# Re-measured durations, overlaps and delays in a kernel's list schedule, with exponentials and sines planned in pieces

## The chip, the cores and the metric

The kernel runs on one core of a Trainium2 chip. Its engines are TensorE (PE in the profile, with PEld for its weight loads), VectorE (DVE), ScalarE (ACT), GpSimd (POOL, which here only issues transfers) and SyncE (SP, which issues the other transfers); 16 DMA engines move the data. The metric is the device time in microseconds (us), as the median of several runs.

## The reference

Two branches over the same 2048 tokens of 512 channels are mixed by a gate for each token.

```python
g = sigmoid((x * gate_w).sum(-1, keepdims=True))
return g * a + (1 - g) * b

# a: a diagonal state-space layer (S4D) as a long convolution, 128 states a channel
dt = exp(log_dt)
A = -exp(log_A_real) + 1j * A_imag
C = (C_real + 1j * C_imag) * dt[:, None]
P = exp((A * dt[:, None])[:, :, None] * arange(2048))
K = 2.0 * einsum("dn,dnl->dl", C, P).real
a = irfft(rfft(u_t, 4096) * rfft(K, 4096))[:, :, :2048] + u * D_skip   # transposed

# b: a bilinear feed-forward layer of 1792 hidden channels
b = ((x @ w_gate) * (x @ w_up)) @ w_down
```

Everything is float32. B_x is not used: both branches take A_u.

## The kernel before, in words

**The feed-forward branch (GLU).** Each float32 factor is split into a rounded high part and a rest (xhi and xlo, whi and wlo, hh and hl, dhi and dlo), and a product is three matmuls, a *triple*, of 128x128 by 128x512 (`product` and `down`). The hidden channels are 14 tiles of 128, in five groups; the tokens are four chunks of 512. For each group and chunk, `hidden` makes a tile: eight triples into the accumulators pg and pu, a copy of pg to h on ACT, h = pu * h on DVE, hh = rounded h on ACT, hl = h - hh on DVE. `down` multiplies hh and hl by the down weights into y, and `evacuate` scales y on ACT into acc, which is added to the output by a transfer that POOL issues. There are 56 hidden steps and 672 triples.

**The state-space branch.** Channels go in 16 blocks of 32. For a block, `amplitudes` makes 21 real exponentials (one ACT operation for each of 21 powers, for two blocks at a time, into the tile e) and `phases` makes sines and cosines: on DVE the phase t, on ACT its rounding rt, on DVE the rest, and on ACT an absolute value and two sines. Their products on DVE (`direct_powers`, `leads`, `x_table`, `v_table`) are tables of powers x and v, whose matmuls on PE (`k_block`, its task `kgen`) give 2048 values of the convolution's kernel for each channel. Both it and the input go through a Fourier transform of two steps made of small matmuls (`u_part`, `k_first`, `m_second`), are multiplied on DVE (`m_product`), and come back in two steps (`m_inverse`, `m_last`), with transfers to memory and back between the steps. Four blocks make a quarter of the channels, after which `transforms` runs for this quarter.

**The order of the work.** Nothing is issued as it is written. Every function adds *tasks* to a list: the engine, a planned duration in us, the instructions, the tiles read and written, a rank (lower goes first), perhaps an earliest time `after`, and for a transfer its size. `Work.run` (lines 216 to 265) is a list scheduler: again and again it takes the task that can start earliest, at equal starts the one of lower rank, then of lower number, and moves the engine's planned time on by the duration. A task can start when its inputs have ended, plus a delay (`inputs`, lines 187 to 195), and when the buffers that it needs have been left by their users, plus the same delay (`slots`). The delay is 0.7 us for a task of PE and 0.15 us for the others, and nothing between two tasks of one engine:

```python
LAG = {"pe": 0.7}
lag = self.LAG.get(task.engine, 0.15)
at = max(at, d.end + (lag if d.engine != task.engine else 0.0))
```

At the end the tasks are issued in that order, and each engine then runs its own in order, whatever the real times are. Planned durations thus decide the order alone. Hidden steps are released one every `T_STEP` = 10.3 us of planned time and have rank 2 on PE; copies and products between them on ACT and DVE have rank 0; the state-space tasks have rank 1, some 0 or -1.

The 21 exponentials are one task of `1.3 + 21 * (0.13 + 0.0021 * 32 * blocks)` us (line 754), and the absolute value and the two sines are one task of 3.6 or 2.3 us (line 776). Exponentials and sines need different tables in ACT, which an ACT_TABLE_LOAD exchanges.

The operations go through one recorder, so that the profile has line 98 for all of them; they are told apart by their tiles (out<-in).

Of the kernel before, what the change touches and what calls it, by code (L numbers as in the profile page):

```python
# [13 lines left out]
AF = mybir.ActivationFunctionType  # L14
# [6 lines left out]
KT = D // P  # L21
# [6 lines left out]
TWO_PI = 2.0 * math.pi  # L28
# [4 lines left out]
NP = len(POWERS)  # L33

TURNS = [-l for l in POWERS[:11]] + POWERS[11:]
TB = 32
# [106 lines left out]
class Work:  # L143
# [7 lines left out]

    LAG = {"pe": 0.7}
    DMA_RATE = 0.3
# [10 lines left out]
    def add(self, engine, us, fn, r=(), w=(), rank=1, after=0.0, dma=0, hold=(), rows=()):  # L164
# [20 lines left out]
        return task  # L185

    def inputs(self, task):

        lag = self.LAG.get(task.engine, 0.15)
        at = task.after  # L190
        for d in task.deps:
            if d.end is None:
                return None
            at = max(at, d.end + (lag if d.engine != task.engine else 0.0))
        return at

    def slots(self, task, at):

        lag = self.LAG.get(task.engine, 0.15)
        taken = {}  # L200
        for tile in task.tiles:
            if tile.made is not None:
                continue
            n = taken.get(tile.key, 0)
            taken[tile.key] = n + 1
            place = len(tile.had) + n
            if not tile.loose and tile.turn != place:
                return None
            if place >= tile.bufs:
                for d in tile.had[place - tile.bufs].users:  # L210
                    if d.end is None:
                        return None
                    at = max(at, d.end + (lag if d.engine != task.engine else 0.0))
        return at

    def run(self):
# [5 lines left out]
        while any(left.values()):  # L222
# [29 lines left out]
            t.start, t.end = start, start + t.us  # L252
            free[t.engine] = t.end
            if t.dma:
# [14 lines left out]
def gated_mix_kernel(  # L269
# [20 lines left out]
    add = work.add  # L290
# [292 lines left out]
    def u_part(c):  # L583
# [159 lines left out]
    def amplitudes(bs):  # L743

        if bs[0]:
            pars.update(parameters(bs))
        par, rates = pars[bs[0]][2]
        e = new("tab", "e", [P, 2 * TB, NP])

        def exps():  # L750
            for k, l in enumerate(POWERS):
                act.activation(e.t[:, : TB * len(bs), k].rearrange("p (n d) -> p n d", d=TB), rates(), AF.Exp, scale=float(l))

        add("act", 1.3 + NP * (0.13 + 0.0021 * TB * len(bs)), exps, r=[par], w=[e])
        for n, b in enumerate(bs):
            amps[b] = e, lambda n=n: e.t[:, TB * n : TB * (n + 1)]

    def phases(b):
# [11 lines left out]

        def sines():
            act.activation(rt.t, t.t, AF.Abs)
            act.activation(t.t, t.t, AF.Sin, scale=-TWO_PI)
            act.activation(rt.t, rt.t, AF.Sin, scale=-TWO_PI, bias=half_pi[:, 0:1])

        add("act", 3.6 if b % 2 or not b else 2.3, sines, r=[m_const], w=[t, rt])
        polar[b] = t, rt
# [19 lines left out]
    def leads(b):  # L797
# [3 lines left out]
        par, C = pars[b][1]  # L801
        add("act", 0.42, lambda: act.copy(x.t[:, :, :, 0], C()), r=[par], w=[(x, ("l", 2))])
        q = new("tab", "sq", [P, 2, 2, TB, 3])
# [57 lines left out]
    def v_table(b):  # L861
# [7 lines left out]

        add("act", 1.3, copies, r=[ri], w=[(v, 2)])  # L870
        outer(
# [4 lines left out]
        for to, of, n in ((32, 0, 16), (56, 32, 8)):  # L876
# [11 lines left out]
            us = 0.04 * n + 0.08  # L888
            add("act", 2 * us - 0.2, sq_act, r=src_parts, w=[(v, ("r", k)), sq])
            add(  # L890
# [11 lines left out]
    def k_block(b, x, v):  # L902
# [26 lines left out]
    def k_first(q, kt):  # L929

        tt(0.19, lambda: kt.t[:, 48, :], lambda: kt.t[:, 48, :], lambda: skip[:, q], ALU.add, [m_skip], [kt])
        for h in range(2):
# [16 lines left out]

            add("pe", 2.1, fn, r=[kt, m_w1k], w=banks, rank=-1, hold=sts)  # L950
            for half in range(2):
# [58 lines left out]
    def m_second(q, ins, w):  # L1010
# [17 lines left out]

        add("pe", 2.1, fn, r=[*ins, w], w=banks[0] + banks[1], rank=1, hold=tos)
        for which in range(2):  # L1030
# [39 lines left out]
    def m_inverse(q, T, y, w):  # L1070
# [13 lines left out]

        add("pe", 1.15, fn, r=[y, w], w=banks, rank=1, hold=[ts])
        for j in range(4):
# [14 lines left out]
    def m_last(q, half):  # L1101
# [30 lines left out]

        add("pe", 1.9, fn, r=src, w=banks, rank=1, hold=fins)
        for i, f in enumerate(banks):
# [14 lines left out]

            args = ("dve", 0.69, mix_dve) if q == KT - 1 else ("act", 1.2, mix_act)  # L1150
            add(*args, r=[f, (m_gate, r // 4)], w=[(fin, i)])
# [119 lines left out]
```

## Time and profile before

| | |
|---|---|
| runs before, median | 632.51 us (631.53 to 634.56, three runs) |
| profiled execution, its own time | 633.44 us |
| its span, first to last instruction | 631.7 us |
| PE busy | 612.6 us, 97% |
| DVE busy | 495.4 us, 78% |
| ACT busy | 399.6 us, 63% |
| mean granted TensorE clock | 0.997 |

The profile is of one execution. Busy time of PE counts from the first to the modelled end of each matmul, and matmuls overlap, so that gaps of up to 0.16 us between matmuls don't show as idle. In the rows, "y<-dhi,hl" is an operation that writes y and reads dhi and hl; "k" is any accumulator of the state-space branch; the number after x is how many instructions a row holds; brackets at the end of a row give the idle time of the engine before it and what ended it, where "issue" means nothing that the profile shows.

### The profile page before, as it was taken

The page shows a single profiled execution, that of the slowest core. Times are in us where ns is not written, and L with a number is a line of the kernel's source. Part 1 is how long each engine was busy: PE and PEld are TensorE (multiplying, and loading weights), DVE is VectorE, ACT ScalarE, POOL GpSimd, SP SyncE. Part 2 cuts the span into 40 slices and gives each one's busy share as a digit, 9 for nine tenths or more (in the row PEclk, how much of TensorE's full clock was granted, in tenths as well). Part 3 has the DMA queues.
Part 4 walks back from the last instruction along what each step waited for, and adds up shares of the span by engine and source line. Part 5 has one row for each costly group of instructions (what it writes and reads, how often), then busy time and mean ns, then how long its engine had stood idle before and what let it go on. Part 6 is the DMA issues. An engine that isn't in the chain of part 4 may idle for free.

```text
span 631.7 us, 18000 instructions
## 1 busy us (share of the span) xinstructions
PE 612.6 (97%) x7526; PEld 468.8 (74%) x7526; DVE 495.4 (78%) x764; ACT 399.6 (63%) x931; POOL 106.1 (17%) x157
## 2 busy tenths in 40 slices
PE   8989999999999999999999999999999999998996
PEld 5667677678688887787778778768887887776783
DVE  6958999989969899799778898977998872146524
ACT  4477877885876795668687765785786543333320
POOL 3231523111021021002110202030101011130101
PEclk9999999999999999999999999999999999999998
DMA  8896949559779599578988959597979699897956
GB/s 309 295 335 248 328 136 369 178 159 287 190 183 300 148 242 274 136 217 190 260 196 199 292 159 247 156 190 190 276 165 265 184 255 252 285 248 206 239 129 116
DMA packets 111893, 142.64 MB, mean 226 GB/s; under 512 B 7876, under 2 KB 66756, under 8 KB 111556
## 3 DMA queue, kind: packets, MB, share of 16 engines
q1 hardware_dynamic: 90100, 105.05, 52.7%
q0 software_dynamic: 21568, 36.45, 28.0%
q8 instruction: 59, 0.97, 0.6%
q14 instruction: 22, 0.18, 0.1%
q10 hardware_dynamic: 144, 0.00, 0.0%
HBM read 81.96 MB, written 59.51 MB: 224 GB/s over the span
## 4 chain that ended last, share of the span: by engine, by line
PE 81%; issue 7%; DVE 5%; DMA 4%; POOL 1%; ACT 1%; POOLq 0%
PE y L98 22%; PE pg L98 20%; PE pu L98 20%; PE k L98 19%; DMA x_d<-xhi 2%; DVE x L98 2%; DMA su_d<-ts 1%; DVE v L98 1%; POOL x_d L98 1%; DMA y<-in_xT 1%; DVE m L98 1%; POOL su_d L98 0%; DVE hl L98 0%; DVE wlo L98 0%; DVE ri L98 0%
## 5 line engine op out<-in xcount | busy, mean ns | idle before, releaser
L98 POOL DMA_DIRECT2D out<-acc x60 | 51.5, 916 | 372.2 <-ACT acc L98 341.7
L98 PE MATMUL y<-dhi,hl 128*128 128x512 f32 x224 | 91.4, 408 | 3.8 <-DVE hl L98 3.5
L98 PE MATMUL pg<-xhi,wlo 128*128 128x512 f32 x224 | 90.3, 403 | 3.6 <-ACT h L98 1.5
L98 PE MATMUL pu<-xhi,wlo 128*128 128x512 f32 x224 | 89.7, 400 | 0.6 <-DVE h L98 0.6
L98 PE MATMUL pg<-xlo,whi 128*128 128x512 f32 x224 | 87.6, 391 | 0.1
L98 PE MATMUL y<-dlo,hh 128*128 128x512 f32 x224 | 87.5, 391 | 0.0
L98 PE MATMUL pg<-xhi,whi 128*128 128x512 f32 x224 | 87.5, 390 | 0.0
L98 PE MATMUL y<-dhi,hh 128*128 128x512 f32 x224 | 87.4, 390 | 0.0
L98 PE MATMUL pu<-xlo,whi 128*128 128x512 f32 x224 | 87.4, 390 | 0.0
L98 PE MATMUL pu<-xhi,whi 128*128 128x512 f32 x224 | 87.3, 390 | 0.0
L98 DVE TENSOR_TENSOR h<-pu,h 128x512 f32<-128x512 f32 x56 | 38.6, 689 | 55.9 <-PE pu L98 36.1
L98 ACT ACTIVATE acc<-y,ngate 128x512 f32<-128x512 f32 x76 | 51.5, 686 | 36.5 <-PE y L98 28.9
L98 ACT CAST hh<-h 128x512 fp32r<-128x512 f32 x56 | 34.7, 621 | 57.5 <-DVE h L98 57.5
L98 ACT COPY ts<-k 128x256 f32<-128x256 f32 (+1 forms) x144 | 51.2, 435 | 21.3 <-PE k L98 21.3
L98 PEld LDWEIGHTS y<-dhi,hl 128*128 128x128 f32 x224 | 42.0, 187 | 24.5 <-issue 7.9
L98 PEld LDWEIGHTS pg<-xhi,wlo 128*128 128x128 f32 x224 | 42.0, 187 | 21.0 <-issue 5.0
L98 ACT COPY h<-pg 128x512 f32<-128x512 f32 x56 | 32.9, 588 | 37.7 <-PE pg L98 25.3
L98 PEld LDWEIGHTS pu<-xhi,wlo 128*128 128x128 f32 x224 | 42.0, 188 | 14.8 <-issue 4.7
L98 PEld LDWEIGHTS y<-dhi,hh 128*128 128x128 f32 x224 | 42.1, 188 | 9.3
L98 PEld LDWEIGHTS pg<-xhi,whi 128*128 128x128 f32 x224 | 42.0, 188 | 9.1
L98 PEld LDWEIGHTS pu<-xhi,whi 128*128 128x128 f32 x224 | 42.1, 188 | 9.1
L98 PEld LDWEIGHTS pg<-xlo,whi 128*128 128x128 f32 x224 | 42.1, 188 | 8.6 <-DVE xlo L98 0.5
(105 smaller groups left out, 1128.6 us busy)
## 6 DMA issues: line engine op xcount, KB each, us to landing
out<-acc POOLq DMA_DIRECT2D x60, 256.0 KB, 6.3
xhi<-x_d SPq DMA_DIRECT2D x48, 256.0 KB, 5.1
xlo<-x_d SPq DMA_DIRECT2D x48, 256.0 KB, 5.2
raw<-in_wts SPq DMA_DIRECT2D x36, 256.0 KB, 4.6
su_d<-ts POOLq DMA_DIRECT2D x32, 256.0 KB, 6.2
sk_d<-ts SPq DMA_DIRECT2D x16, 512.0 KB, 5.7
y_d<-ts SPq DMA_DIRECT2D x16, 512.0 KB, 5.0
in<-sk_d SPq DMA_DIRECT2D x12, 512.0 KB, 7.4
```

What stands on the lines that cost most here:

```text
L98: got = getattr(self.engine, name)(*args, **kw)
```

## The change

No instruction is added, removed or altered; only the planner's numbers and the size of some tasks change, and with them the order. A dependence now costs nothing between two tasks of PE; otherwise 0.06 us for a task of PE, 0.3 for one of SP or POOL and 0.03 for ACT and DVE (now also behind a task of the same engine), and 0.17 more behind a task of PE. ACT and DVE are taken to be free 0.09 and 0.08 us before a task's end. The durations of PE's tasks and of some of ACT's are new. The 21 exponentials become three tasks of seven, and the absolute value and the two sines three tasks.

```diff
-    LAG = {"pe": 0.7}
+    LAG = {"pe": 0.06, "sp": 0.3, "pool": 0.3}
+    PE_LAG = 0.17
+    OVERLAP = {"act": 0.09, "dve": 0.08}
...
+    def ready(self, task, d):
+        if d.engine == task.engine == "pe":
+            return d.end
+        return d.end + self.LAG.get(task.engine, 0.03) + (self.PE_LAG if d.engine == "pe" else 0.0)
...
-            at = max(at, d.end + (lag if d.engine != task.engine else 0.0))
+            at = max(at, self.ready(task, d))
...
-            free[t.engine] = t.end
+            free[t.engine] = t.end - self.OVERLAP.get(t.engine, 0.0)
...
-        add("pe", 0.69, fn, r=[(w[0], which), (w[1], which), x[0], x[1]], w=[pg], rank=2, after=after)
+        add("pe", 0.681, fn, r=[(w[0], which), (w[1], which), x[0], x[1]], w=[pg], rank=2, after=after)
...
-        add("pe", 0.69, fn, r=[*h, *w], w=[y], rank=2)
+        add("pe", 0.681, fn, r=[*h, *w], w=[y], rank=2)
...
-        add("pe", 2.0, fn, r=[ut, m_w1], w=banks[0] + banks[1], rank=1, hold=sts)
+        add("pe", 2.08, fn, r=[ut, m_w1], w=banks[0] + banks[1], rank=1, hold=sts)
...
-        def exps():
-            for k, l in enumerate(POWERS):
-                act.activation(e.t[:, : TB * len(bs), k].rearrange("p (n d) -> p n d", d=TB), rates(), AF.Exp, scale=float(l))
-        add("act", 1.3 + NP * (0.13 + 0.0021 * TB * len(bs)), exps, r=[par], w=[e])
+        def exps(ks):
+            for k in ks:
+                act.activation(
+                    e.t[:, : TB * len(bs), k].rearrange("p (n d) -> p n d", d=TB), rates(), AF.Exp, scale=float(POWERS[k])
+                )
+        for n in range(3):
+            ks = range(7 * n, 7 * n + 7)
+            add("act", 0.17 + 1.29 * (n == 0) + 7 * (0.09 + 0.0009 * TB * len(bs)), lambda ks=ks: exps(ks), r=[par], w=[(e, n)])
...
-        add("act", 3.6 if b % 2 or not b else 2.3, sines, r=[m_const], w=[t, rt])
+        add("act", 0.77, lambda: act.activation(rt.t, t.t, AF.Abs), r=[t], w=[rt])
+        add(
+            "act", 2.13 if b % 2 or not b else 0.83, lambda: act.activation(t.t, t.t, AF.Sin, scale=-TWO_PI), w=[t],
+        )
+        add(
+            "act", 0.83, lambda: act.activation(rt.t, rt.t, AF.Sin, scale=-TWO_PI, bias=half_pi[:, 0:1]), r=[m_const],
+            w=[rt],
+        )
...
-        add("pe", 2.07, kgen, r=[x, v], w=[pk], rank=0, hold=[kt])
+        add("pe", 2.15, kgen, r=[x, v], w=[pk], rank=0, hold=[kt])
```

The other tasks of PE go from 2.1 to 2.08 (`k_first`), from 2.1 to 2.13 (`m_second`), from 1.15 to 1.27 (`m_inverse`) and from 1.9 to 2.0 (`m_last`); three more of ACT's fall by 0.02 to 0.11 us, and the two pairs of squares go from 1.24 and 0.6 to 1.15 and 0.73.

More of the change, by code (lines that the diff above doesn't have):

```diff
@@ L212, in slots @@
                         return None
-                    at = max(at, d.end + (lag if d.engine != task.engine else 0.0))
+                    at = max(at, self.ready(task, d))
         return at
@@ L801, in leads @@
         par, C = pars[b][1]
-        add("act", 0.42, lambda: act.copy(x.t[:, :, :, 0], C()), r=[par], w=[(x, ("l", 2))])
+        add("act", 0.31, lambda: act.copy(x.t[:, :, :, 0], C()), r=[par], w=[(x, ("l", 2))])
         q = new("tab", "sq", [P, 2, 2, TB, 3])
@@ L868, in copies @@
                 act.copy(v.t[:, c, :, 49:56], ri.t[:, c, :, W_A])
-        add("act", 1.3, copies, r=[ri], w=[(v, 2)])
+        add("act", 1.28, copies, r=[ri], w=[(v, 2)])
         outer(
@@ L888, in v_table @@
             us = 0.04 * n + 0.08
-            add("act", 2 * us - 0.2, sq_act, r=src_parts, w=[(v, ("r", k)), sq])
+            add("act", 1.15 if n == 16 else 0.73, sq_act, r=src_parts, w=[(v, ("r", k)), sq])
             add(
@@ L948, in fn @@
                     to += n
-            add("pe", 2.1, fn, r=[kt, m_w1k], w=banks, rank=-1, hold=sts)
+            add("pe", 2.08, fn, r=[kt, m_w1k], w=banks, rank=-1, hold=sts)
             for half in range(2):
@@ L1027, in fn @@
                                 )
-        add("pe", 2.1, fn, r=[*ins, w], w=banks[0] + banks[1], rank=1, hold=tos)
+        add("pe", 2.13, fn, r=[*ins, w], w=banks[0] + banks[1], rank=1, hold=tos)
         for which in range(2):
@@ L1083, in fn @@
                             )
-        add("pe", 1.15, fn, r=[y, w], w=banks, rank=1, hold=[ts])
+        add("pe", 1.27, fn, r=[y, w], w=banks, rank=1, hold=[ts])
         for j in range(4):
@@ L1131, in fn @@
                     )
-        add("pe", 1.9, fn, r=src, w=banks, rank=1, hold=fins)
+        add("pe", 2.0, fn, r=src, w=banks, rank=1, hold=fins)
         for i, f in enumerate(banks):
```

8 lines of the change are left out of this document (1 added, 7 removed).

## The prediction

> **What bounds the kernel now.** I read the page first, for the engines' shares and the chain.
>
> ```profile
> span 631.7 us, 18000 instructions
> ...
> PE 612.6 (97%) x7526; PEld 468.8 (74%) x7526; DVE 495.4 (78%) x764; ACT 399.6 (63%) x931; POOL 106.1 (17%) x157
> ...
> PE 81%; issue 7%; DVE 5%; DMA 4%; POOL 1%; ACT 1%; POOLq 0%
> ```
>
> TensorE (PE) is busy 97% of the span and holds 81% of the chain, so time can only come from gaps on PE. The second view, busy time by stretches, says where they are.
>
> ```profile
> 50.00:100.00 50.00, 48.18 (x324) 35.38 (x323) 46.62 (x79) 39.84 (x87) 15.49 (x24) 1.00 0.67 239
> 100.00:150.00 50.00, 48.73 (x446) 36.21 (x445) 46.19 (x75) 39.77 (x89) 10.05 (x14) 1.00 0.70 229
> 250.00:300.00 50.00, 50.00 (x676) 38.67 (x668) 44.49 (x60) 35.96 (x89) 5.83 (x6) 1.00 0.71 183
> 500.00:550.00 50.00, 50.00 (x538) 38.30 (x528) 23.12 (x35) 20.51 (x47) 4.12 (x5) 1.00 0.90 260
> ```
>
> The columns are PE, weight load, DVE (VectorE), ACT (ScalarE) and POOL. Early, PE lacks 1 to 2 us in 50, while DVE is at 92%; later PE is full, and the granted clock is 1.00 throughout. The chain and the timeline then give the exact size of a gap. In a full stretch twelve matmuls take 2.72 us, 0.227 us from start to start, although each is recorded 0.39 long; so a gap is the distance of two starts less 0.227, and is 0.16 us more than the idle time printed.
>
> ```profile
> 608.30 2.72 PE pg L98 x12
> ...
> 620.72 5.00 PE y L98 x21
> ```
>
> I went through the starts of all matmuls. After the first 20 us the gaps over 0.4 us are of two kinds. Seven, all before 170 us, end with a result of DVE or ACT. Five, later, end with nothing that the profile names; they lie inside or beside blocks of very many small matmuls, such as these:
>
> ```profile
> 376.64 0.43 PE L98 MATMUL k<-v,x 128*32 128x64 f32 x10 [0.56 <-issue]
> ...
> 584.76 0.69 PE L98 MATMUL k<-y,w3s 32*64 32x128 f32 x29 [1.46 <-issue]
> ...
> q8 instruction: 59, 0.97, 0.6%
> ```
>
> PE has 2 x 7526 instructions and queue q8 carried 59 blocks of them, one per some 255; a block of 128 small matmuls with 128 weight loads uses one up in 2 us. That the five gaps (0.84, 1.19, 0.76, 1.41, 1.71 us; 5.9 in all) are late instruction blocks is a reading, not shown. No planned duration changes how many instructions PE runs, so I leave them as they are.
>
> **The change part by part.** The program adds no arithmetic and takes none away; the same instructions are issued in another order. So every part is worth what it does to the seven gaps, and to gaps that are not there yet.
>
> First the exponentials in pieces. The largest gap:
>
> ```profile
> 108.48 0.69 DVE L98 TENSOR_TENSOR h<-pu,h 128x512 f32<-128x512 f32 x1 [0.56 <-PE pu L98]
> ...
> 109.68 1.28 ACT L98 ACT_TABLE_LOAD   x1
> 110.97 3.27 ACT L98 ACTIVATE e<-pb 128x64 f32<-128x64 f32 x21
> 114.07 0.61 ACT L98 CAST hh<-h 128x512 fp32r<-128x512 f32 x1
> ...
> 113.74 1.09 DVE L98 TENSOR_TENSOR x<-m,x 128x896 f32<-128x896 f32 x1
> ...
> 116.88 0.68 DVE L98 TENSOR_TENSOR hl<-h,hh 128x512 fp32r<-128x512 f32 x1
> ...
> 115.97 0.39 PE L98 MATMUL pu<-xhi,whi 128*128 128x512 f32 x1
> ...
> 117.62 0.50 PE L98 MATMUL y<-dhi,hl 128*128 128x512 f32 x1 [1.26 <-DVE hl L98]
> ```
>
> h is ready at 109.17, yet its rounding hh is queued on ACT behind the whole block of exponentials, 1.28 + 3.27 = 4.6 us; then hl is queued on DVE behind three products of 1.1 us, and PE waits 117.62 - 115.97 - 0.227 = 1.42 us. The plan had put that block at 1.3 + 21 x (0.13 + 0.0021 x 64) = 6.9 us, so it saw hh and hl 2.3 us later than they were. The new pieces sum to 0.17 x 3 + 1.29 + 21 x (0.09 + 0.0009 x 64) = 4.9 us, and hh, of rank 0, may cut in after the first seven (110.97 + 7 x 0.147 = 112.0). hl then stands at 113.74 at the latest, 3.1 us sooner, and PE needs it 1.4 sooner: the gap goes, **1.42 us**. The other gap of this kind:
>
> ```profile
> 160.19 3.27 ACT L98 ACTIVATE e<-pb 128x64 f32<-128x64 f32 x21
> ...
> 163.86 0.61 ACT L98 CAST hh<-h 128x512 fp32r<-128x512 f32 x1
> ...
> 167.13 0.39 PE L98 MATMUL pu<-xhi,whi 128*128 128x512 f32 x1
> ...
> 168.29 0.50 PE L98 MATMUL y<-dhi,hl 128*128 128x512 f32 x1 [0.77 <-DVE hl L98]
> ```
>
> It is 168.29 - 167.13 - 0.227 = **0.93 us**, and goes for the same reason. The other exponential blocks stand where PE had other matmuls queued and nothing waited; splitting them brings nothing.
>
> The Trainium skill speaks against splitting: ScalarE: Activation LUTs (Table sets: the hidden batching unit) advises running all calls of one table set together, and puts a switch at about 2.66 us, 1.28 for the load and 1.38 for a drain. By that figure one sine between two pieces would cost 5.3 us of ACT.
>
> What a switch costs here is in these rows:
>
> ```profile
> 126.36 1.28 ACT L98 ACT_TABLE_LOAD   x1
> 127.66 0.76 ACT L98 ACTIVATE t<-t 128x672 f32<-128x672 f32 x1
> ...
> L98 ACT ACT_TABLE_LOAD x20 | 25.7, 1283 | 2.8 <-DMA pb<-par_d 1.3 <-PEq L1260 1.2
> ```
>
> The sine starts 20 ns after the load ends, so a switch is 1.28 us and nothing more. The sines of a block run at 127.7, 13 us behind its exponentials, because two DVE passes lie between; the list puts pieces that are ready at once in order of their number, so I expect 20 loads again and count nothing. Sines in three pieces follow the same reasoning: 0.77 + 2.13 (or 0.83) + 0.83 planned against 0.77 + 1.28 + 0.77 + 0.84 in rows, and a rank-0 copy may go between.
>
> Next the delays and overlaps: an engine's input 0.15 us behind another's end becomes 0.03, DVE and ACT are free 0.08 to 0.09 us before an operation's end. A gap that these made:
>
> ```profile
> 30.47 0.62 ACT L98 CAST hh<-h 128x512 fp32r<-128x512 f32 x1 [2.27 <-DVE h L98]
> ...
> 31.07 0.39 PE L98 MATMUL pu<-xhi,whi 128*128 128x512 f32 x1
> ...
> 31.57 0.69 DVE L98 SCALAR_TENSOR_TENSOR y<-in,bd 128x512 f32<-128x512 f32 x1
> ...
> 32.18 0.69 DVE L98 TENSOR_TENSOR hl<-h,hh 128x512 fp32r<-128x512 f32 x1
> ...
> 32.92 0.50 PE L98 MATMUL y<-dhi,hl 128*128 128x512 f32 x1 [1.46 <-DVE hl L98]
> ```
>
> hh ends at 31.09, and DVE still does a score product ahead of hl. One place sooner is 32.18 - 31.57 = **0.61 us** of the 1.62. At 75 us the copy h stands behind an acc that came in at 75.84:
>
> ```profile
> 75.51 0.39 PE L98 MATMUL pu<-xhi,whi 128*128 128x512 f32 x1
> ...
> 75.84 0.70 ACT L98 ACTIVATE acc<-y,ngate 128x512 f32<-128x512 f32 x1
> 76.42 0.60 ACT L98 COPY h<-pg 128x512 f32<-128x512 f32 x1
> ...
> 77.07 0.50 PE L98 MATMUL pg<-xhi,wlo 128*128 128x512 f32 x1 [1.17 <-ACT h L98]
> ```
>
> pg was done by 75.2; one place is 76.42 - 75.84 = **0.58** of 1.33. Three smaller gaps (0.61, 0.49, 0.71 at 36, 45 and 62 us) sum to 1.8; I take half, **0.9**, between none and all.
>
> PE's durations (0.69 to 0.681, kgen 2.07 to 2.15 and so on) shorten the planned GLU by 672 x 0.009 = 6 us and lengthen the rest; the hidden steps are still released every 10.3 us. A GLU step needs 12 x 0.681 = 8.2 of these, so PE has little room either way: nothing counted.
>
> Last the part that can cost: PE's margin of 0.7 us behind another engine's result becomes 0.06. That is what the hardware does: hl ends at 32.87 and PE starts at 32.92. But the margin was also what kept PE from waiting after 170 us.
>
> ```profile
> 158.79 0.42 DVE L98 TENSOR_TENSOR v<-v,sq 128x256 f32<-128x256 f32 x1
> ...
> 159.78 0.64 PE L98 MATMUL k<-v,x 128*32 128x64 f32 x29
> ...
> L98 DVE TENSOR_TENSOR ri<-t,e 128x672 f32<-128x672 f32 x16 | 13.6, 851 | 0.0
> ```
>
> Here kgen starts 0.57 us after its table is ready; over the 16 kgens that slack runs from 0.57 to 9.9 us, and is under 2 us in eleven. Taking 0.64 from each leaves most with some. The cost lies between nothing and 11 x 0.64 = 7 us; I take **1.0**, near the low end, because even the tightest row nearly covers it, and because after one wait PE is late against its plan, which pays for the next.
>
> Sum: 1.42 + 0.93 + 0.61 + 0.58 + 0.9 - 1.0 = 3.4 us. The profiled execution took 633.44 (its span 631.7 and 1.7 around), 0.9 over the median of 632.51; 3.4 less is 630.0 for such an execution and **629.1** for the median. The end is not touched: from the last y matmul (625.7) on it is one product, one add and one transfer, 6.0 us.
>
> **The rivals.** (1) *The gaps move.* The list is made anew from the first microseconds on, and another copy or product may end up behind another block. For it: the five smaller terms rest on one place in a queue. Against: both large gaps have one cause that the change takes away. With only these two gone and the 1.0 paid, 632.5 - 2.35 + 1.0 = 631.2: no change. (2) *The margin was worth more than the gaps.* Place: PE's first matmul of each kgen and each inverse, where DVE delivers last. The new plan keeps 0.83 us for DVE operations that take 0.851 (row above), five in each block, so DVE is planned about 0.1 us fast per block where the old one planned it slow by 0.08 us an operation. If DVE's lateness exceeds the 0.06 at each kgen, each waits some 0.3 us (half of the 0.64 taken away) and restarts with a first matmul of 0.50 instead of 0.39 us: 16 x 0.41 = 6.6 us. Less the two large gaps: 632.5 - 2.35 + 6.6 = 636.8, slower. It decides from the point where DVE, at 92%, is the last to arrive at PE's head of queue; after 500 us, with DVE at 46%, it cannot. (3) *Parted tables.* A sine falls between two pieces of exponentials. Each time is two loads more, 2 x 1.28 = 2.6 us of ACT; in the three blocks before 170 us, where ACT delays show, 3 x 2.6 = 7.7, so 632.5 - 1.1 + 7.7 = 639. The 13 us between them speak against it. (This is where the rule of the Trainium skill's page ScalarE: Activation LUTs would bite.)
>
> **How the numbers follow.** Forecast 0.43, rival 1 0.33, rival 2 0.21, rival 3 0.03. About 0.5% (3.2 us) is what a measurement of this kernel can tell from no change: the three runs before spread over 3.0 us. The forecast lies just past that bound, 629.1 against 629.3: about a third of its cases would end above it, and about as many of rival 1, those in which more than the two gaps close, below. So faster 0.43, same 0.33, slower 0.24. The forecast's own range is 625 to 631.5. All seven gaps closed (7.1 us) and one late instruction block less (1.2) gives 624.2, the low end; rival 2 with half a microsecond more gives the high end, 637.5.
>
> **What would show it.** Right: no exponential row of 21 in one piece, hh within 3 us of h, no gap of 1 us before 170 us; 20 table loads; five or so unnamed gaps of 6 us together, and no PE wait for DVE or ACT above 0.5 us after 170. Wrong: PE waits for DVE v or y rows ahead of kgen or inverse blocks (rival 2), more than 22 loads (rival 3), or the same sum of early gaps in other places (rival 1).

## The result, and the profile after

The changed kernel takes 643.59 us in the median (642.85 to 647.32, four runs); beside them the kernel before took 632.63 (four runs). The ratio is 1.0161, with a 95% interval of 1.0123 to 1.0200: 11 us slower, where 629.1 was predicted and 637.5 was the upper end of the range. The profiled execution of the changed kernel took 644.3 us, that of before 633.44.

The page of the changed kernel, its span, its engines and its chain:

```profile
span 642.5 us, 17987 instructions
...
PE 615.5 (96%) x7526; PEld 471.1 (73%) x7526; DVE 485.3 (76%) x764; ACT 399.0 (62%) x931; POOL 106.2 (17%) x157
...
PE 87%; DMA 5%; issue 3%; DVE 2%; ACT 2%; SPq 1%; ACTq 0%; DVEq 0%
```

The instruction counts of the five engines are those of before. PE holds 87% of the chain (81% before), so the 10.8 us of span are looked for on PE. Its idle time rose from 19.1 to 27.0 us (span less busy time) and its busy time from 612.6 to 615.5. First the places where the prediction looked: busy time by stretches (PE, PEld, DVE, ACT, POOL, then clock, DMA share, GB/s).

```profile
50.00:100.00 50.00, 49.01 (x326) 35.24 (x327) 45.81 (x83) 39.84 (x88) 16.87 (x27) 1.00 0.82 267
100.00:150.00 50.00, 50.00 (x456) 39.05 (x455) 48.94 (x80) 40.87 (x90) 9.80 (x14) 1.00 0.61 209
```

The early gaps are smaller: between 100 and 150 us PE has none left (48.73 before). The timeline at the gap that the prediction put first:

```profile
107.67 2.25 ACT L98 ACTIVATE e<-pb 128x64 f32<-128x64 f32 x14
...
111.91 1.20 ACT L98 ACTIVATE e<-pb 128x64 f32<-128x64 f32 x7
...
114.43 0.69 DVE L98 TENSOR_TENSOR h<-pu,h 128x512 f32<-128x512 f32 x1
115.15 0.62 ACT L98 CAST hh<-h 128x512 fp32r<-128x512 f32 x1
116.23 0.68 DVE L98 TENSOR_TENSOR hl<-h,hh 128x512 fp32r<-128x512 f32 x1
```

The block of 21 is parted, and hh follows h at once (115.15 behind 114.43 + 0.69), where before it stood behind 4.6 us of exponentials. The loss lies elsewhere. The view of PE's waits lists what ended PE's idle times: us in total, times, longest. Of the kernel before, the rows without a name:

```profile
PE k L98 <- issue: 3.6, 4, 1.5
...
PE pg L98 <- issue: 1.2, 1, 1.2
```

and of after, with the largest named one:

```profile
PE k L98 <- issue: 12.3, 10, 3.4
PE y L98 <- DVE hl L98: 3.7, 2, 2.9
...
PE y L98 <- issue: 1.1, 1, 1.1
...
PE pg L98 <- issue: 1.0, 1, 1.0
PE pu L98 <- issue: 0.7, 1, 0.7
```

Idle time that ends with nothing the profile names went from 4.8 us (5 times) to 15.1 us (13 times). Named idle time stayed the same in sum: 8.0 us before, 7.9 after (all other rows of the view added up). From start to start, as the prediction measured them, the unnamed gaps are 5.9 and 17.9 us; the expectations below also count unnamed gaps from start to start, and so give more than the view (16.9 and 17.9 us where it has 15.1). The last matmul starts at 638.09 us instead of 625.32, 12.8 later; the unnamed gaps are 12.0 of it, and a stretch at half the granted clock at the start (below) adds 2.4 that the view doesn't count as idle, against some 1.6 of smaller gaps that are no longer there. The tail behind that matmul fell from 6.3 to 4.4 us, which leaves 10.9 (10.8 between the rounded spans).

**What an unnamed gap is.** I numbered PE's instructions in the order of their start: matmuls, weight loads and, between them, the instructions for semaphores (104 before, 94 after) and three drains. Each of these gaps, in both kernels, lies ahead of an instruction whose number is 193 or 194 plus a multiple of 256. Queue q8, which moves instructions, shows one transfer of 16 KiB for each such block (59 in each kernel). The longest of after, in the timeline:

```profile
473.78 1.31 PE L98 MATMUL k<-v,x 128*32 128x64 f32 x78
478.49 0.46 PE L98 MATMUL k<-v,x 128*32 128x64 f32 x17 [3.39 <-issue]
```

and four blocks as worked out from the trace (when PE entered the block, how many of its 256 instructions belong to the small matmuls of the state-space branch, when the transfer on q8 for the following block ran, when PE entered that one):

```
entered   small   transfer of the next      next entered
266.39     230    263.32 - 264.20           271.05   no gap
416.78     222    417.41 - 418.57           422.29   no gap
441.75     252    443.41 - 444.39           445.79   gap of 1.74 at 444.02
471.98     249    476.07 - 477.00           478.49   gap of 3.59 at 474.88
```

The transfer takes about 1 us (0.9 to 1.9), but in the changed kernel starts anywhere from 4.9 us before to 6.3 us after PE enters the block ahead of it, and at the 13 gaps PE goes on 1.3 to 1.6 us after it ends. A block of GLU matmuls lasts some 29 us (entered at 596.82, the next at 625.83) and hides all this; one of small matmuls can be used up in 2 to 4 us and may not. The profiles of the runs below agree: in none of the sixteen does PE enter a block less than 1.1 us after its transfer has ended. What sets the start of a transfer is not shown. Over all 944 transfers of the sixteen profiles it comes later with more traffic: 0.7 us (median) behind PE's entry into the block ahead where the DMA engines were less than half busy, 2.3 us where they were at least 95% busy (in the 3 us from the moment when PE is 64 instructions short of that block). Whether the traffic is the cause was not tested.

The Trainium skill (Runtime: NRT & Kernel Launch, Instruction fetch mechanics) says that instructions come in blocks of 256 while the current block executes and that crossing a boundary is mostly hidden. The 256 agree with this trace; "mostly hidden" does not, with 15.1 us of idle time at these boundaries.

**Why there are more of them.** Busy time of PE alone by stretches, before:

```profile
200.00:250.00 50.00, 49.36 (x841) 1.00 0.87 223
300.00:350.00 50.00, 49.01 (x781) 1.00 0.86 222
450.00:500.00 50.00, 50.00 (x1024) 1.00 0.85 211
550.00:600.00 50.00, 47.30 (x911) 1.00 0.96 229
```

and after (from 20 to 50 us PE was busy 27.89 us before, at a clock of 1.00):

```profile
20.00:50.00 30.00, 26.32 (x98) 0.89 0.78 250
200.00:250.00 50.00, 47.02 (x1050) 1.00 0.87 230
300.00:350.00 50.00, 47.57 (x947) 1.00 0.99 253
450.00:500.00 50.00, 45.90 (x664) 1.00 0.81 234
550.00:600.00 50.00, 48.85 (x289) 1.00 0.85 176
```

The same 7526 matmuls, but in another order: 1050 and 947 in two stretches that held 841 and 781, and few left after 550 us (289 for 911). The number in a stretch of 50 us doesn't decide: from 450 to 500 us the kernel before ran 1024 without a gap, and the changed one 664 with 4.1 us lost. What counts is how the small ones fall into blocks. Blocks in which at least 240 of 256 instructions are small rose from 4 to 13, and each of the 13 gaps lies behind a block with at least 230. A dense block is not always late: of the 4 before, one had a gap behind it, of the 13 after, nine.

**The start.** The row of 20 to 50 us shows a clock of 0.89. The timeline there:

```profile
20.32 0.39 PE L98 MATMUL y<-dhi,hh 128*128 128x512 f32 x1
...
21.23 0.68 DVE L98 TENSOR_TENSOR h<-pu,h 128x512 f32<-128x512 f32 x1
...
22.89 0.68 DVE L98 TENSOR_TENSOR hl<-h,hh 128x512 fp32r<-128x512 f32 x1
...
23.63 0.79 PE L98 MATMUL y<-dhi,hl 128*128 128x512 f32 x1 [2.93 <-DVE hl L98]
24.22 0.63 PE L98 MATMUL y<-dlo,hh 128*128 128x512 f32 x1
24.65 0.63 PE L98 MATMUL y<-dhi,hh 128*128 128x512 f32 x1
```

The new plan has hl end at 20.52 us and so puts y ahead of the next step's pg, by 0.02 us; the chip ends hl at 23.57. PE waits, and the next dozen matmuls start 0.43 us apart instead of 0.227, some 2.4 us more. The granted clock is 0.50 from 22.75 to 29.57 us, so it fell 2.0 us after PE had gone idle. The Trainium skill (TensorE: Matmul & The Clock Gate, Part 1) has the clock halved after an idle window of about 3.4 us whose phase runs free of the program. A phase of its own can be why 3.39 us idle at 474 us brought no half clock (stretch 450 to 500 at 1.00), but that it takes 3.4 us idle does not agree with the traces: 2.93 us were enough here, and 1.89 us in e11_late_loads below (idle to 532.43 us, clock 0.50 from 532.7 to 536.1).

### The profile page after: what moved, and what is told of

It reads as the page before. It is cut to its first block, busy times and chain, and to the rows that moved or that the text cites. A ratio compares the mean times of both kernels' runs of the same rounds, so it can differ in the third digit from the quotient of the medians.

```text
span 642.5 us, 17987 instructions
## 1 busy us (share of the span) xinstructions
PE 615.5 (96%) x7526; PEld 471.1 (73%) x7526; DVE 485.3 (76%) x764; ACT 399.0 (62%) x931; POOL 106.2 (17%) x157
## 4 chain that ended last, share of the span: by engine, by line
PE 87%; DMA 5%; issue 3%; DVE 2%; ACT 2%; SPq 1%; ACTq 0%; DVEq 0%
PE y L98 23%; PE pg L98 23%; PE pu L98 22%; PE k L98 20%; DMA raw<-in_wts 2%; DMA pb<-par_d 1%; DVE x L98 1%; DMA small<-in_rows 1%; ACT ts L98 1%; DMA raw<-in_xT 1%; SPq L98 1%; DVE hl L98 0%; ACT e L98 0%; DVE kt L98 0%; ACT acc L98 0%
## 5 line engine op out<-in xcount | busy, mean ns | idle before, releaser
L98 ACT CAST hh<-h 128x512 fp32r<-128x512 f32 x56 | 34.7, 620 | 48.4 <-DVE h L98 48.1
```

What stands on the lines that cost most here:

```text
L98: got = getattr(self.engine, name)(*args, **kw)
```

## The experiments

One table first. "Unnamed" and "named" are PE's idle times in the view of waits, summed, of the one profiled execution, whose own time stands beside it; it is not always near the median, so the medians decide and the idle times say where. "Clock" is the mean granted TensorE clock of that execution. Each row is named by the label that its expectation has. "Before" is the kernel before on the same chip beside them; the changed kernel itself was timed in the first session only (643.59 beside 632.63), so differences between rows that stand beside different "before" are good to the 1.5 us by which these differ.

| run | edit | median us (range, n) | before | ratio [95%] | profiled us | unnamed | named | clock |
|---|---|---|---|---|---|---|---|---|
| e1_shift | after, 112 more PE instructions at the start | 644.25 (642.33-647.82, 4) | 633.63 | 1.0175 [1.0136, 1.0214] | 642.33 | 13.1 | 7.4 | 0.992 |
| e2_after_blocks | after, instruction blocks planned | 628.93 (627.32-629.77, 4) | 633.63 | 0.9931 [0.9906, 0.9955] | 627.32 | 1.8 | 6.5 | 0.997 |
| e3_before_blocks | before, instruction blocks planned | 631.59 (630.43-632.85, 10) | 633.63 | 0.9963 [0.9945, 0.9980] | 630.98 | 3.1 | 7.4 | 0.994 |
| e4_margin | after, PE's delay 0.7 | 636.62 (631.56-640.50, 10) | 633.63 | 1.0040 [1.0010, 1.0070] | 631.56 | 5.7 | 8.6 | 1.000 |
| e5_blocks_late_loads | e2, transfers planned from 2.5 us | 625.70 (625.57-628.25, 4) | 633.79 | 0.9850 [0.9787, 0.9912] | 625.76 | 1.9 | 8.0 | 1.000 |
| e6_whole | after, no pieces | 646.78 (646.52-650.29, 4) | 633.79 | 1.0184 [1.0117, 1.0252] | 650.29 | 14.3 | 8.3 | 0.984 |
| e7_no_overlap | after, no overlaps | 637.59 (634.02-640.74, 10) | 633.79 | 1.0045 [1.0011, 1.0080] | 634.02 | 3.6 | 7.4 | 0.993 |
| e8_old_delays | after, old delays | 632.02 (628.52-635.02, 10) | 633.79 | 0.9950 [0.9908, 0.9991] | 630.15 | 5.8 | 5.2 | 1.000 |
| e9_pieces | before, with the pieces | 627.95 (625.73-629.45, 6) | 634.12 | 0.9874 [0.9827, 0.9921] | 629.45 | 4.8 | 6.0 | 0.999 |
| e10_pe_margin | before, PE's delay 0.06 | 645.33 (641.72-649.06, 6) | 634.12 | 1.0159 [1.0108, 1.0210] | 649.06 | 11.5 | 12.1 | 0.989 |
| e11_late_loads | after, transfers planned from 2.5 us | 651.59 (647.08-653.03, 6) | 634.12 | 1.0238 [1.0188, 1.0288] | 653.03 | 18.0 | 7.7 | 0.987 |
| e12_blocks_whole | e5, no pieces | 628.84 (627.53-631.17, 9) | 634.12 | 0.9911 [0.9878, 0.9944] | 631.17 | 1.0 | 10.3 | 0.993 |
| e13_margin_blocks | e10, instruction blocks planned | 646.72 (641.51-649.77, 6) | 633.00 | 1.0208 [1.0161, 1.0254] | 645.37 | 6.1 | 12.4 | 0.989 |
| e14_pieces_blocks | e9, instruction blocks planned | 625.37 (625.10-628.29, 6) | 633.00 | 0.9888 [0.9846, 0.9930] | 625.42 | 0.2 | 5.2 | 0.998 |

**Theory and rivals.** Theory: the loss is late instruction blocks, brought about by an order with denser blocks. Rivals: the lost margin, in named waits (the prediction's rival 2); the start alone. Few of the expected times were met, and the counts of dense blocks that several rest on did not give the size: 8 in e6_whole came with 14.3 us of unnamed idle time, 10 in e11_late_loads with 18.0, the 13 of the changed kernel with 15.1.

### Moving the block boundaries (e1_shift)

The order stays (behind the warm-up all matmuls, and all 931 operations of ACT, stand as they did); one of three warm-up matmuls becomes 29 small ones, which changes nothing that is kept and shifts every boundary by 112 instructions.

```diff
-            for _ in range(3):
+            for _ in range(2):
...
+            for k in range(29):
+                c = k % 4 * 32
+                pe.matmul(
+                    scratch.t[c : c + 32, :64], zero.t[:, c : c + 32], zero.t[:, :64], start=True, stop=True,
+                    tile_position=(0, c),
+                )
```

> The changed kernel with its order untouched. One of the three warm-up matmuls at the start (12 instructions of PE) becomes 29 small ones on zeros, so that every later instruction of PE stands 112 places further on, and the 256-instruction blocks are cut elsewhere. Theory (PE runs out of instructions: in the changed kernel the gaps that the profile names after nothing, 16.9 us, all lie at the entry of a block): the gaps move, and where the cuts now fall fewer blocks consist of small matmuls alone. An estimate fitted to both traces (a block can be entered 5 to 6 us after PE came within 48 to 80 instructions of the one before) gives 9.2 us for the changed kernel, where 16.9 were measured, and 3.2 here, so about 6 us here: 643.6 - 11 = 633, at least under 638. Rival (PE waits for results that come too late, since its margin was taken away): the same waits at the same matmuls, 643.6 within 1.5.

644.25 us. The gaps left their matmuls and came at others, again all at numbers 193 or 194 of a block, fewer (7 for 13) but longer. The longest of the shifted kernel:

```profile
202.78 0.73 PE L98 MATMUL k<-v,x 128*32 128x64 f32 x37
207.31 0.22 PE L98 MATMUL k<-v,x 128*32 128x64 f32 x1 [3.81 <-issue]
```

So the gaps are bound to the blocks and not to tiles, buffers or the work around them. The size was missed (633 expected): other cuts through the same order cost as much. The run also has 6.8 us at half clock behind two of these gaps.

### Planning the instruction blocks (e2_after_blocks, e3_before_blocks)

The planner counts PE's instructions and lets a task that enters a new block start no sooner than 7.0 us after the moment when PE was 64 instructions short of the block ahead of it; so it puts GLU matmuls between the dense ones. Each task of PE carries its number of instructions (`ins`: 6 for a triple, 256 for `kgen` and so on, times 1.007 for the semaphore waits).

```diff
+    BLOCK, ENTRY, AHEAD, FETCH = 256, 194, 64, 7.0
...
+    def block(self, task, start):
+        n, late = self.pe[-1][0], 0.0
+        b = self.ENTRY + self.BLOCK * math.ceil((n - self.ENTRY) / self.BLOCK)
+        while b < n + task.ins:
+            at = b - self.BLOCK - self.AHEAD
...
+            asked = t0 + (t1 - t0) * (at - n0) / max(n1 - n0, 1e-9)
+            late = max(late, asked + self.FETCH - start - task.us * (b - n) / task.ins)
+            b += self.BLOCK
+        return start + late
...
+                if t.engine == "pe":
+                    start = self.block(t, start)
```

> The changed kernel, whose planner now also counts PE's instructions: a task may not enter a block of 256 sooner than 7 us after PE came within 64 instructions of the block before; where it would, another task (nearly always GLU matmuls) goes first. Durations, delays, overlaps and pieces are those of the change. Theory (late blocks cost 16.9 us): nearly all of them go, 643.6 - 16 = 628, and the gaps that remain are those of the first 70 us. Rival (the lost margin): waits for DVE and ACT stay, over 640.

> The kernel before, with the same count of instructions in its planner and nothing else. Theory: its five late blocks (5.9 us) go, 632.6 - 5.9 = 627. Rival (those five gaps were something else, or the order gets worse elsewhere by as much): 631 to 636.

On the changed kernel 628.93, 14.7 us below 643.59; the waits of this kernel:

```profile
PE y L98 <- DVE hl L98: 3.4, 2, 2.8
PE k L98 <- issue: 1.8, 4, 0.9
```

From profile to profile the time fell by 17.0 us (644.3 to 627.32), and 13.3 of them are unnamed idle time (15.1 to 1.8); the wait at 20 us stayed. On the kernel before it brought 2.0 us: 631.59, where 627 was expected and the rival had 631 to 636. The unnamed idle time fell only from 4.8 to 3.1 us there, and the three gaps left stand at block entries again: they are late blocks that the plan did not catch, and not something else, as the rival had it. The run on the changed kernel is the main evidence for the theory: all of the change's durations, delays and pieces stand, and with the blocks spread they make a kernel that is faster than before. It also reorders, so it doesn't prove the size of each gap.

### Each part undone on the changed kernel (e4, e6, e7, e8)

PE's delay back at 0.7 (e4):

```diff
-    LAG = {"pe": 0.06, "sp": 0.3, "pool": 0.3}
+    LAG = {"pe": 0.7, "sp": 0.3, "pool": 0.3}
```

The 21 exponentials, and the absolute value and the two sines, back in one task each, with durations that are the sums of the pieces (e6):

```diff
+        add("act", 0.51 + 1.29 + NP * (0.09 + 0.0009 * TB * len(bs)), exps, r=[par], w=[e])
...
+        add("act", 3.73 if b % 2 or not b else 2.43, sines, r=[m_const], w=[t, rt])
```

ACT and DVE free at the end of a task and not before it (e7):

```diff
-            free[t.engine] = t.end - self.OVERLAP.get(t.engine, 0.0)
+            free[t.engine] = t.end
```

All delays between tasks as in the kernel before, while overlaps, durations and pieces stay (e8):

```diff
-    LAG = {"pe": 0.06, "sp": 0.3, "pool": 0.3}
-    PE_LAG = 0.17
+    LAG = {"pe": 0.7}
...
-            at = max(at, self.ready(task, d))
+            at = max(at, d.end + (lag if d.engine != task.engine else 0.0))
```

> The changed kernel with one number back: 0.7 us instead of 0.06 for PE behind another engine's result. Rival 2 of the prediction (the margin itself was worth the time): back to 632 or below, with the waits of PE for DVE and ACT gone. Late blocks: here too the small matmuls lie less densely (the estimate is 4.0 us against 9.2 for the changed kernel, that is some 7 measured against 16.9), 643.6 - 9.5 = 634, but what has gone are gaps at block entries, and waits for DVE and ACT stay about as they are.

> The changed kernel with exponentials and sines as whole tasks again, with the new durations (their pieces' sums). The order then has 8 blocks of at least 240 instructions of small matmuls of 256, against 13 in the changed kernel and 4 before, and hl of the second step is again placed ahead of its release. Theory (late blocks and the start): blocks cost about 10 us and not 17.9, the start stays: 643.6 - 8 = 636. Rival (the pieces are what costs, by ACT's order): 632 or less, with the late blocks as many as in the changed kernel.

> The changed kernel without the overlaps of ACT and DVE. 5 blocks of at least 240 small; the y matmuls of the second step stand behind the third step's first matmuls. Theory: late blocks some 7 us (less 10) and the start regained (less 5): 629. Rival (the overlaps as such are right and do not matter): 641 or more.

> The changed kernel with all its delays as before (0.7 us for PE, 0.15 for the others, none within an engine). 4 blocks of at least 240 small, 18 of at least 230 (the changed kernel has 21); the start as before. Theory: late blocks some 8 us (less 10), the start regained (less 5): 629. Rival 2 of the prediction (the margin of PE was what kept it from waiting): 632 or less as well, but then late blocks stay at 17 us and what goes are waits for DVE and ACT after 70 us, of which the changed kernel has next to none.

With the old delays 632.02, 11.6 us below the changed kernel (629 expected; the unnamed idle time fell to 5.8 us, where the rival had it stay): the delays are the part that costs. PE's margin alone put back takes 7.0 off (636.62), the overlaps left out 6.0 (637.59). Both missed (634 and 629 expected). In e7 late blocks did go (3.6 us unnamed, 1.9 of them at the last projection and not at a block's entry), and its last matmul starts at 620.31, 17.8 us sooner than in the changed kernel, but the last projection comes last there and the tail is 11.9 us instead of 4.4. Without the pieces 646.78, where 636 was expected from fewer dense blocks; its interval overlaps that of the changed kernel, so this says only that the pieces don't cause the loss. The parts don't add up, as each edit makes another order.

### Each part alone on the kernel before (e9, e10)

The pieces with the change's durations for them, nothing else (e9; the sines likewise, as in the change's diff):

```diff
-        add("act", 1.3 + NP * (0.13 + 0.0021 * TB * len(bs)), exps, r=[par], w=[e])
+        for n in range(3):
+            ks = range(7 * n, 7 * n + 7)
+            add("act", 0.17 + 1.29 * (n == 0) + 7 * (0.09 + 0.0009 * TB * len(bs)), lambda ks=ks: exps(ks), r=[par], w=[(e, n)])
```

PE's delay, nothing else (e10):

```diff
-    LAG = {"pe": 0.7}
+    LAG = {"pe": 0.06}
```

> The kernel before with nothing but the exponentials in three tasks of seven and the absolute value and sines in three tasks, planned with the change's durations; all delays as before. The prediction's step (the gaps of 1.42 and 0.93 us at 116 and 167 us go): 2.35 us faster, near 631.4 where the kernel before has 633.8. Block theory: in the issued order, counted from the program, blocks of 256 PE instructions that consist almost wholly of small matmuls fall from 4 to 1, so the unnamed gaps stay below 6 us and nothing is lost: 630 to 632. Rival (the pieces are part of the loss, because they let the state-space branch run earlier): 636 or more.

> The kernel before with nothing but PE's planned delay behind another engine cut from 0.7 to 0.06 us. The prediction's step (this margin costs 1.0 us, in waits for DVE and ACT): 634.8 where the kernel before has 633.8, the loss in named waits. Block theory: the blocks that are almost wholly small matmuls rise from 4 to 10, so the loss is in unnamed gaps at every 256th instruction, 4 to 6 us more of them: 638 to 640. Rival 2 of the prediction: named waits of 6.6 us ahead of kgen and inverse blocks, 640.

The pieces alone make the kernel 6.2 us faster, 627.95, better than any of the expectations. Its waits:

```profile
PE k L98 <- issue: 3.6, 5, 1.1
...
PE y L98 <- DVE hl L98: 1.5, 1, 1.5
...
PE pg L98 <- issue: 1.2, 1, 1.2
```

Of the seven early gaps, those at 45, 62, 75, 116 and 167 us are gone (0.49 + 0.71 + 1.33 + 1.43 + 0.93 = 4.9 us); those at 31 and 36 stay, the second grown from 0.59 to 1.15 us. Exponentials and sines were not parted one without the other, so how much each gave is open. The unnamed idle time is 4.8 us, as before.

The margin alone makes it 11.2 us slower, 645.33. Its waits have both kinds of loss:

```profile
PE k L98 <- issue: 10.6, 7, 3.3
PE pg L98 <- ACT h L98: 6.3, 3, 4.3
```

The named one, in the timeline:

```profile
44.72 0.39 PE L98 MATMUL pu<-xhi,whi 128*128 128x512 f32 x1
...
48.22 0.62 ACT L98 CAST xhi<-raw 128x512 fp32r<-128x512 f32 x1 [4.37 <-DMA raw<-in_xT]
48.74 0.58 ACT L98 COPY h<-pg 128x512 f32<-128x512 f32 x1
49.38 0.79 PE L98 MATMUL pg<-xhi,wlo 128*128 128x512 f32 x1 [4.27 <-ACT h L98]
```

ACT, in order, waits 4.37 us for a load of x that the plan must have had in sooner; the copy h is queued behind it and PE waits for h, then runs at half clock (0.63 us matmuls up to 53 us, granted clock 0.50 from 47.76 to 54.58). This isn't rival 2's place: no row waits ahead of kgen or the inverse.

### The start alone, and the late loads (e5, e11)

```diff
-        bus, order, known, rows = 0.0, [], {}, {}
+        bus, order, known, rows = 2.5, [], {}, {}
```

> The changed kernel with the count of instruction blocks, and one more number: the planned time from which the transfers are queued starts at 2.5 us and not at 0. In the changed kernel the planner has hl of the second hidden step end at 20.52 and puts its y matmuls at 20.58, 0.02 us ahead of the third step's release at 20.6; on the chip the down weights land 2 to 3 us later than planned, hl is late, PE stands 3.1 us and then runs at half clock for 2 us. With later planned loads the pg matmuls go first. Theory (two causes: late blocks, and this one place at the start): 628.9 - 5 = 624, the gap at 20 us gone and the granted clock 1.0 between 20 and 50 us. Rival (the start is made up for later, since the order is bound elsewhere): 628 to 630.

> The changed kernel with nothing but the planner's transfers starting at 2.5 instead of 0 us, no count of instruction blocks. If the start is a term by itself, the 3.1 us wait at 20 us and the half clock behind it go and the unnamed gaps stay: 638 to 640. If the start only moved with the rest, 643 to 644. Counted from the program, blocks almost wholly of small matmuls are 10 instead of 13, so some unnamed gaps may go too, down to 636.

On top of the planned blocks it brings 3.2 us (628.93 to 625.70; 624 expected): the wait at 20 us and its half clock are gone. By itself it is 8 us worse than the changed kernel, 651.59, against every expectation. Its waits:

```profile
PE k L98 <- issue: 14.7, 8, 2.7
PE pu L98 <- issue: 3.3, 2, 1.9
```

The wait at 20 us is gone here too, but the order after it is another one, with 18.0 us of late blocks. So the start is a real term, but it can't be read off by an edit in this kernel while the blocks are left to chance.

### Pieces and margin with the blocks planned (e12, e13, e14)

> The planner of the fastest run so far (changed kernel, instruction blocks counted, transfers from 2.5 us, 625.7 us) with the 21 exponentials and the two sines as single tasks of the same total duration. If the pieces are worth what the prediction gave them (2.35 us): 628. If their gain only shows where the order was otherwise the old one: 625.7 within 1.5. No unnamed gaps of over 4 us in all in either case.

> The kernel before with PE's planned delay cut from 0.7 to 0.06 us, and the planner counting PE's instruction blocks as in the earlier runs. The cut alone gave 645.3 us; its profile had 13.8 us of unnamed gaps, 7.8 more than before, and 6 to 10 us more of named waits and half clock. If the unnamed gaps are late blocks and the larger half of the loss: they fall below 4 us and the time to 632 to 636. If the loss lies in the named waits for ACT and DVE and the unnamed gaps only go with it: 640 or more.

> The kernel before with the exponentials and sines in pieces (628.0 us alone, with 6.4 us of unnamed gaps in its profile) and the planner counting PE's instruction blocks, delays as before. If the unnamed gaps are late blocks that the count avoids: 3 to 5 us less, 623 to 625. If the margin of 0.7 us already spreads the small matmuls enough, so that what is left is chance: 627 to 628.

e12 is e5 with the whole tasks of e6; e13 and e14 are e10 and e9 with the block count of e3. Their edits are the lines shown above, joined. With blocks planned, the pieces are worth some 3.1 us (628.84 against 625.70, two ratios whose intervals overlap at the edge), in named waits and the half clock that follows; the waits of the whole one:

```profile
PE pg L98 <- ACT h L98: 5.2, 2, 3.9
```

In the longest of them the copy h stands on ACT, at 48.34 us, behind a table load and both sines (from 45.06 us on), so the sines in one task are what delays it.

The margin's loss does not go with the late blocks: 646.72. Unnamed idle time fell from 11.5 to 6.1, but the early waits stay:

```profile
PE pg L98 <- ACT h L98: 6.3, 3, 4.3
PE k L98 <- issue: 3.2, 3, 2.4
```

and the tail grew: the last matmul starts at 632.76 (642.86 in e10's profile), but the last projection is now nearly last in the list, and the run ends 10.8 us behind that matmul (4.4 in e10). The output of the last projection (out<-ts, on queue q0 by the trace until 641.0 us) still moves when the last of the other outputs (out<-kt, until 641.8) do; in the changed kernel q0 was done at 619.9:

```profile
631.58 2.87 POOL L98 DMA_DIRECT2D out<-ts  x2 [27.05 <-DVE ts L98]
...
634.89 3.12 SPq L98 DMA_DIRECT2D out<-kt  x4
```

So for the margin alone late blocks are one part of the loss and early waits another; how much of it each is in the median stays open, since e10 and e13 have one profiled execution each and their runs spread over 7 to 8 us. For the whole change, where the pieces had taken most of those early waits away, the blocks are the bulk (e2).

e14 is the kernel before with pieces and blocks: 625.37 us, 1.1% faster than before, like e5 the fastest. Whether the blocks add to the pieces is not settled: with pieces alone it was 627.95 and the unnamed idle time fell from 4.8 to 0.2 us, but beside their own kernels before the two ratios are the same (0.9888 and 0.9874). Its page:

```profile
span 623.7 us, 17979 instructions
...
PE 610.0 (98%) x7526; PEld 468.6 (75%) x7526; DVE 495.1 (79%) x764; ACT 400.7 (64%) x931; POOL 106.3 (17%) x157
```

## Why the prediction was wrong

**Right: the exponentials.** "The gap goes, 1.42 us" and the 0.93 behind it: both went, in the changed kernel and with the pieces alone, and the pieces alone gave 6.2 us where these terms summed to 2.35. (The prediction calls the gap of 1.42 us the largest; its own lists have 1.62 and 1.71.) The gaps at 45, 62 and 75 us, which I had put down to delays and overlaps (0.58 and half of 1.8), went with the pieces too. 20 table loads were expected and 20 came; the profile groups of the changed kernel:

```profile
L98 ACT ACT_TABLE_LOAD x20 | 25.7, 1283 | 1.5 <-PEq L1275 1.2
```

So rival 3 did not come into play. The rule of the Trainium skill's page ScalarE: Activation LUTs (Table sets: the hidden batching unit) against parting one set's calls did not bite either, as the same row shows 20 loads of 1.283 us. The sines in pieces, which the sum put at nothing, were worth something too (e12).

**Wrong, the first step: the five unnamed gaps.** "No planned duration changes how many instructions PE runs, so I leave them as they are." The count is fixed, but what a block costs depends on what stands in it, and the order is just what planned times change. The reading was right (late blocks) and its consequence was not drawn: 4.8 us of idle time became 15.1. This is the step that decided the sign: with the blocks planned and all else of the change kept, the kernel takes 628.93 us (e2). The profile of before had the signs: five gaps "inside or beside blocks of very many small matmuls", and a block of 256 small instructions gone in 2 us.

**Wrong, the second step: the margin.** "The cost lies between nothing and 11 x 0.64 = 7 us; I take 1.0, near the low end." Alone it cost 11.2 us, beyond the bound. I priced it at kgen and the inverse, in PE's waits for DVE after 170 us. There it was indeed next to nothing: after 170 us the changed kernel shows no wait of PE for DVE or ACT above 0.5 us, as the prediction said. The margin did two other things: it kept dense tasks apart, and it left room for loads that land later than planned. Neither was in the sum.

**Wrong, the start.** The prediction began its list of gaps at 20 us and had none there; a new one of 3.1 us with 2.4 us of half clock came, from an order decided by 0.02 us in the plan. "No gap of 1 us before 170 us" fell there, and again with a late block at 166 us (1.02 us idle).

**The rivals.** Rival 1 (gaps move) is the closest in kind, but the gaps that moved in were late blocks. Rival 2 had the sign, at 636.8, and the wrong place: its waits ahead of kgen and inverse never came. The range ended at 637.5 because it was built from rows of named waits alone, and even so left out its own rival 3, put at 639; the 4.8 us that PE waits for "issue" should have had a bound of its own, above as well as below. The share "issue" in the chain is no measure of it: it fell from 7% to 3% while these gaps grew, since most of it before (34.7 of 47 us) lies in four stretches of the first 61 us in which PE has no unnamed gap at all.

**The end.** "The end is not touched": the tail fell from 6.3 to 4.4 us, a gain of 1.9 that the sum lacked. The likely reason is that the last projection's transfers on q0 end at 619.9 instead of 629.0 us and no longer run beside the last ones. In the ten of the sixteen profiles in which q0 is done before the last matmul starts, the tail is 4.4 us; in the six others it is 6.3 to 11.9 (the longest in e7 and e13). No run moved that projection alone.

## What to carry to other kernels

Before trusting a better cost in a list scheduler, ask what its old slack covered beside the thing it was named for: here 0.7 us of "delay" also spread dense code and absorbed late loads, and the honest 0.06 lost 11 us. An idle time that the profile leaves unnamed deserves a bound of its own in both directions, above all when an order is remade; count the instructions of the engine up to each gap, and numbers that differ by multiples of a block (256 here) show an instruction block. Where a resource is not in the plan, single edits measure the shuffle: put it into the plan first, then the other terms show more clearly; e13, whose tail moved, shows that an order remade can still hide one.

## What was not expected of the hardware

- PE's instructions arrive in blocks of 256, one transfer of about 1 us on q8 each, started between 4.9 us before and 6.3 us after PE enters the block ahead (changed kernel); where PE had to wait, it went on 1.3 to 1.6 us after the transfer had ended. A stretch of some 250 small matmuls and weight loads lasts 2 to 4 us, and one boundary behind such a stretch cost up to 3.6 us in the changed kernel and 4.0 in e1 (3.81 idle).
- An idle PE of 2.93 us (changed kernel) and one of 4.27 us (e10) each came with 6.8 us of half clock (0.43 instead of 0.227 us from start to start once PE ran again), one of 1.89 us (e11) with 3.4 us, and one of 3.39 us (changed kernel, 474 us) with none. The length of the idle time alone does not decide.
- Runs of one kernel spread differently: 9 us over ten runs in e4 (5.7 us unnamed in its profile), 2.4 us over ten runs in e3, where the blocks are planned, but 8.3 us over six in e13, where they are planned too. What makes the spread is open.
